# First double pair's q, k, v in a tile outside the pool that later holds odd batches' rows; SyncE's loads and stores also in the planned order

## The chip, the cores and the metric

One core of a Trainium2 chip. The time is device microseconds of one execution; the kernel before takes 632.27 us, median of 3 runs (630.27 to 633.63). TensorE multiplies matrices, ScalarE applies tanh and exp, VectorE adds, transposes in 32x32 blocks and normalises, GpSimd casts weights and gathers and scatters rows, SyncE issues the plain DMA transfers.

## The reference

```python
def _attn_ref(q, k, v, cap):                      # 8 batches, 12 heads, 448 rows, 64 wide
    scores = np.matmul(q, k.transpose(0, 1, 3, 2)) / np.sqrt(q.shape[-1])
    scores = cap * np.tanh(scores / cap)
    attn = np.exp(scores - np.max(scores, axis=-1, keepdims=True))
    attn = attn / (np.sum(attn, axis=-1, keepdims=True) + 1e-09)
    return np.matmul(attn, v)

def _moe_ref(x, w_gate, w1, w2, capacity):        # x: 8 x 448 x 768, w1 768 x 1024, w2 1024 x 768
    scores = np.einsum('bsd,d->bs', x, w_gate)
    out = x.copy()
    for b in range(B):
        top_idx = np.argpartition(-scores[b], capacity)[:capacity]      # 128 of 448 rows
        xe = x[b, top_idx]
        ye = np.maximum(xe @ w1, 0.0) @ w2
        g = 1.0 / (1.0 + np.exp(-scores[b, top_idx]))
        out[b, top_idx] = x[b, top_idx] + g[:, None] * ye
    return out
```

All arrays are float32. The attention output with its heads joined is x of the second part.

## The kernel before

The work on heads is cut into 24 "doubles" of two pairs of heads each, three doubles to a batch. A double has q and k tiles of 128 x 448 for each pair (lines 268 to 271), one v tile (273 to 275), and runs in 7 steps over 64 rows of k. A step is four scores products into a PSUM tile ps (L283), tanh on ScalarE into p (L321), exp in place (L324), four products of p with v into acc (L291), and an add of p into e on VectorE (L334). At a double's end TensorE sums e over partitions (sums, L368), VectorE transposes acc and the sums (L360, L376), takes reciprocals, normalises into xn, which holds a batch's rows (L406), and reduces the gate's scores (L428, L432). SyncE stores xn to the output in four transfers after a batch's second and again after its third double (L421). A float32 product shows as two matmul records in the trace, so a step of four scores products counts as x8.

When a batch's three doubles are done, VectorE and TensorE rank its 448 gate scores and pick 128 rows; GpSimd gathers them from the output (L550), the expert products run on TensorE in three parts each (L616, w1 then w2, split in high and low parts), and GpSimd scatters the result (L675). The weights come once, in 14 transfers into three staging tiles (L245), are cast by GpSimd (L248) and split by VectorE (L251).

A planner sets the order: each piece of work is a task with an engine, an assumed duration, a priority, and slots that it takes and gives (SIZES: 2 for "qk", 3 for "v", 2 for "S" in PSUM, 7 for "P", 2 for "xn"). `Plan.run` plays the tasks through and emits instructions in the order in which they would begin. Expert products are used as filling between attention steps; once no more than RESERVE = 42000 ns of them are left they are held until the attention products are done. On TensorE, ScalarE, VectorE and GpSimd the instructions stand in the order emitted (`manual_schedule`); SyncE's are not in that list before, and the tile framework's own scheduler orders them by priority and by when it expects the tiles to be free. On each engine instructions start in order, and SyncE's transfers wait in one line for the semaphores of the tiles that they overwrite.

The first double's loads are issued before the branch on the cap (`tc.If`), from the same pool and tags (`q0`, `k0`, ... with two buffers, `v` with three) as those of all later doubles.

Of the kernel before, what the change touches and what calls it, by code (L numbers as in the profile page):

```python
# [9 lines left out]
F32 = mybir.dt.float32  # L10
# [160 lines left out]
def load_flag(tc, K, cap):  # L171
    nc = tc.nc
    cp = K.const
    K.cap = cp.tile([P, 1], F32, name="capc")
    nc.sync.dma_start(K.cap, cap.to_broadcast([P, 1]))
    K.ident = cp.tile([P, P], F32, name="ident")
    make_identity(nc, K.ident)
    K.fast = cp.tile([1, 1], I32, name="fast")
    sq = cp.tile([1, 1], F32, name="sq")
    nc.vector.tensor_tensor(sq, K.cap[:1], K.cap[:1], op=ALU.mult)  # L180
    nc.vector.tensor_scalar(K.fast, sq, CAP_FAST * CAP_FAST, None, op0=ALU.is_le)
    K.sc = cp.tile([P, 1], F32, name="sc")
    nc.vector.reciprocal(K.sc, K.cap)
    nc.vector.tensor_scalar_mul(K.sc, K.sc, 1.0 / float(K.D) ** 0.5)
    nc.scalar.activation(sq, sq, AF.Tanh)
    K.wts = {}
    for nm, n, m in (("w1", K.ND, K.F), ("w2", K.NF, K.DM)):
        for part in "hl":
            K.wts[nm + part] = cp.tile([P, n, m], F32R, name=nm + part)
    K.wg = cp.tile([P, K.NG, 2, Q], F32, name="wg")  # L190
    K.iota = cp.tile([P, P], F32, name="iota")
    K.ids = cp.tile([P, K.NCH], F32, name="ids")
    K.vals = [cp.tile([P, 4, K.NCH], F32R, name=f"vals{i}") for i in range(2)]
    K.score = [cp.tile([P, K.NCH], F32, name=f"score{i}") for i in range(2)]
    K.rk = [cp.tile([P, K.NCH], F32, name=f"rk{i}") for i in range(2)]
    K.before = cp.tile([P, K.NCH * P], BF16, name="before")
    K.fold = cp.tile([P, 4, Q], F32, name="fold")
    K.ones = cp.tile([P, HD], F32, name="ones")
    K.hs = cp.tile([P, 1024], F32, name="hs")


def load_consts(tc, K):
# [57 lines left out]
class Double:  # L260
# [5 lines left out]

    def load_qk(self, tc, K, h, slot):
        for nm, src in (("q", K.q), ("k", K.k)):
            t = K.work.tile([P, K.S], F32, tag=f"{nm}{h}", name=nm, bufs=2)
            getattr(self, nm)[h] = t  # L270
            tc.nc.sync.dma_start(t, src[self.d, h])  # L271

    def load_v(self, tc, K, slot):
        self.v = K.work.tile([P, K.S // HD, 2, HD], F32, tag="v", name="v", bufs=3)
        tc.nc.sync.dma_start(self.v, K.v[self.d])


# [19 lines left out]
    D.acc = K.psV.tile([P, 2, 512], F32, tag="V", name="acc", bufs=1)  # L297


def attention_tasks(tc, K, D, loaded):  # L300
    nc = tc.nc
    add, S, NS = K.plan.add, K.S, K.NS
    g0 = D.d * NS
    lqk, lv = loaded
    if lqk is None:
        lqk = add("SP", 2400, lambda t: [D.load_qk(tc, K, h, t.got["qk"]) for h in range(2)],
                  prio=g0 - 12, take=("qk",), lat=3500)
        lv = add("SP", 700, lambda t: D.load_v(tc, K, t.got["v"]), prio=g0 - 11, take=("v",),
                 lat=4500)
    pv = prev = ex = None  # L310
    qks = []
    for s in range(NS):
        g = g0 + s
        box = {}

        def qk(t, s=s, box=box):
            box["ps"] = scores_mm(tc, K, D, s, t.got["S"])

        def tanh(t, s=s, box=box):
            D.P[s] = w_tile(K, [P, 2, S], F32, "P", t.got["P"], "p")  # L320
            nc.scalar.activation(D.P[s], box["ps"][:, :, :S], AF.Tanh, scale=K.sc)  # L321

        def exp(t, s=s):
            nc.scalar.activation(D.P[s], D.P[s], AF.Exp, scale=K.cap)  # L324

        def product(t, s=s):
            if s == 0:
                new_acc(K, D)
            attend(tc, K, D, s)

        def sum2(t, s=s):
            if s == 1:
                D.E = w_tile(K, [P, 2, S], F32, "E", t.got["E"], "e")
            nc.vector.tensor_tensor(D.E, D.P[0] if s == 1 else D.E, D.P[s], op=ALU.add)  # L334

        a = add("PE", 752, qk, [lqk], prio=g, take=("S",), mode="att",
                give=[("qk", lqk)] if s == NS - 1 else ())
        qks.append(a)
        blk = g // 2 * 4
        th = add("ACT", 1030, tanh, [a], prio=blk, take=("P",), give=[("S", a)])  # L340
        ex_ = add("ACT", 1075, exp, [th], prio=blk + 1)
        pv_ = add("PE", 752, product, [ex_, lv, pv], prio=g + 1.5, mode="att",
                  take=("V",) if s == 0 else (),
                  give=[("v", lv)] if s == NS - 1 else ())
        if s == 0:
            first_pv, first_th, first_ex = pv_, th, ex_
        else:
            sm_ = add("DVE", 1065, sum2, [ex_, prev if s > 1 else first_ex], prio=g + 2,
                      take=("E",) if s == 1 else ())
            done = add("NONE", 0, lambda t: None, [sm_, pv_], prio=-100, give=[("P", th)])  # L350
            if s == 1:
                first_sum = sm_
                add("NONE", 0, lambda t: None, [sm_, first_pv], prio=-100,
                    give=[("P", first_th)])
            prev = sm_
        pv = pv_
# [33 lines left out]
def output_tasks(tc, K, D, x, rc):  # L390
# [5 lines left out]
    def normalise(t):  # L396
        if grp == 0:
            K.xn_slot[b] = t
            K.xn[b] = w_tile(K, [P, NB, NG, 2, Q], F32, "xn", t.got["xn"], "xn")
            K.part[b] = w_tile(K, [P, NG, NB], F32, "part", t.got["xn"], "part")  # L400
        xn = K.xn[b][:, :, grp].rearrange("p b r d -> p r b d")
        xT = D.xT.rearrange("p r (b d) -> p r b d", d=Q)
# [340 lines left out]

def fast_path(tc, K, first, w1, w2):
    plan = K.plan
    weights(tc, K, w1, w2)
    for d in range(K.B * K.NG):
        D = first if d == 0 else Double(K, d)
        if d == 0:
            loaded = []  # L750
            for key in ("qk", "v"):
                loaded.append(plan.add("SP", 0, lambda t: None, prio=-1000, take=(key,),
                                       lat=1500))
        else:
            loaded = (None, None)
        x, rc = attention_tasks(tc, K, D, loaded)
        output_tasks(tc, K, D, x, rc)
        end_batch(tc, K, D)
    warm = K.bank(1)
    for _ in range(WARM):  # L760
        tc.nc.tensor.matmul(warm[:, :P], lhsT=K.ident, rhs=K.ident, start=True, stop=True)
    load_consts(tc, K)
    load_gate(tc, K)

    def after_attention():
        plan.free["bank"] += [2, 3, 4]

    plan.run(after_attention)
# [10 lines left out]
def main_kernel(ctx: ExitStack, tc: tile.TileContext, q, k, v, cap, w_gate, w1, w2, out, C, dims):  # L779
# [28 lines left out]
    K.bank = bank  # L808
    load_flag(tc, K, cap)
    first = Double(K, 0)  # L810
    first.load_qk(tc, K, 0, 0)
    first.load_qk(tc, K, 1, 0)
    first.load_v(tc, K, 0)
    fast = nc.values_load(K.fast[0:1, 0:1], min_val=0, max_val=1)
    with tc.If(fast > 0) as cmp:
        if C <= P:
            K.plan = Plan(SIZES)
            engines = {mybir.EngineType.PE, mybir.EngineType.Activation, mybir.EngineType.DVE,
                       mybir.EngineType.Pool}
            with tc.manual_schedule(engines=engines):  # L820
                fast_path(tc, K, first, w1, w2)
        else:
# [72 lines left out]
```

## Time and profile before

| what | value |
|---|---|
| runs of the kernel before | 630.27, 633.63, 632.27 us |
| profiled execution | 629.62 us |
| span of its instructions | 627.9 us |
| mean granted clock of TensorE | 0.906 of full speed |
| busy: TensorE, VectorE, ScalarE, GpSimd | 519.0, 399.6, 349.0, 41.2 us |
| moved by DMA | 57.41 MB |

The page gives busy shares per engine, the span in 40 slices, the chain of work that ended last and the costliest groups of instructions. In the views of the trace, a row of the timeline has the start in us from the span's start, the duration in us, engine, line, operation, output and inputs, the count of merged instructions, and in brackets the idle time before it with what ended it. SPq is SyncE's queue of transfers, PEld the weight loads of TensorE. Ends of matmuls are modelled and overlap the next start, so TensorE's pace is read from starts.

### The profile page before, as it was taken

The numbers are of one execution on the slowest core, as the hardware profiler recorded it, in microseconds if no ns is written. First come the engines' busy times: TensorE is split into PE (matmuls) and PEld (weight loads), VectorE is DVE, ScalarE is ACT, GpSimd is POOL, SyncE is SP. The second block draws the span as 40 slices with busy tenths as digits, with TensorE's granted clock in tenths as the row PEclk, the third lists the DMA queues.
The fourth block names the chain that finished last, engine by engine and source line by source line (L and its number), as shares of the span: only waits on it lengthen the run. The fifth ranks groups of instructions, "written<-read, shape, count | busy, mean of one in ns | idle before, by whom it ended". The sixth has DMA issues, their size and how long they took to land.

```text
span 627.9 us, 9365 instructions
## 1 busy us (share of the span) xinstructions
PE 519.0 (83%) x3750; PEld 262.4 (42%) x3750; DVE 399.6 (64%) x671; ACT 349.0 (56%) x394; POOL 41.2 (7%) x40
## 2 busy tenths in 40 slices
PE   6586975979779889799699789896799798795996
PEld 2131322524434435345254333353345344333896
DVE  2879465868576666696287574593748846868621
ACT  5766664638546563676466384663558556690110
POOL 1421001000010000200001000010000000010100
PEclk9888776979898898999799797897979989996999
DMA  7436333151331530342222432115313244103110
GB/s 241 171 110 182 83 105 111 54 143 36 112 99 40 148 89 31 109 130 76 60 88 82 117 77 72 58 58 167 88 33 89 71 128 116 62 25 80 42 45 29
DMA packets 50659, 57.41 MB, mean 91 GB/s; under 512 B 17968, under 2 KB 44720, under 8 KB 50608
## 3 DMA queue, kind: packets, MB, share of 16 engines
q1 hardware_dynamic: 49328, 50.44, 28.0%
q0 software_dynamic: 1280, 6.29, 3.0%
q8 instruction: 31, 0.51, 0.3%
q14 instruction: 20, 0.16, 0.1%
HBM read 42.57 MB, written 14.16 MB: 90 GB/s over the span
## 4 chain that ended last, share of the span: by engine, by line
PE 60%; DMA 16%; DVE 10%; issue 6%; SPq 4%; ACT 2%; POOLq 0%; DVEq 0%
PE ps L283 20%; PE pb L616 18%; PE acc L291 16%; DMA k<-in_k 15%; DVE e L334 5%; SPq L271 4%; PE sums L368 3%; PE pb L579 2%; DMA stage<-in_moe_w 1%; ACT p L321 1%; DVE xn L406 1%; DVE xT L360 1%; DVE sm L376 1%; PE pb L470 1%; ACT p L324 1%
## 5 line engine op out<-in xcount | busy, mean ns | idle before, releaser
L283 PE MATMUL ps<-q,k 64*64 64x448 f32 x1344 | 207.8, 600 | 80.8 <-DMA k<-in_k 79.0
L321 ACT ACTIVATE p<-ps,sc 128x896 f32<-128x896 f32 x168 | 165.9, 1005 | 185.8 <-PE ps L283 169.2
L291 PE MATMUL acc<-p,v 64*64 64x448 f32 x1344 | 180.9, 580 | 1.6 <-ACT p L324 0.6
L324 ACT ACTIVATE p<-p,capc 128x896 f32<-128x896 f32 x168 | 169.9, 1042 | 1.7
L334 DVE TENSOR_TENSOR e<-e,p 128x896 f32<-128x896 f32 x120 | 133.0, 1108 | 39.4 <-ACT p L324 34.1
L283 PEld LDWEIGHTS ps<-q,k 64*64 64x64 f32 x1344 | 62.8, 145 | 188.5 <-issue 103.1
L291 PEld LDWEIGHTS acc<-p,v 64*64 64x64 f32 x1344 | 54.7, 140 | 80.4 <-issue 56.3
L360 DVE STREAM_TRANSPOSE xT<-acc 128x896 f32<-128x896 f32 x24 | 26.7, 1112 | 56.8 <-PE acc L291 52.2
L368 PE MATMUL sums<-e,ones 64*64 64x448 f32 x192 | 27.5, 585 | 14.0 <-DVE e L334 14.0
L550 POOL DMA_INDIRECT xe<-out,idx x8 | 13.1, 1632 | 386.3 <-DVE gt L556 386.3
L376 DVE STREAM_TRANSPOSE sm<-sums 128x896 f32<-128x896 f32 x24 | 26.5, 1103 | 14.0 <-PE sums L368 14.0
L616 PE MATMUL pb<-w2h,hh 128*128 128x384 f32 x128 | 30.5, 356 | 1.1 <-DVE hl L586 1.1
L637 ACT ACTIVATE hs<-pb 128x512 f32<-128x512 f32 x16 | 9.4, 594 | 38.5 <-PE pb L616 38.4
L616 PE MATMUL pb<-w2h,hl 128*128 128x384 f32 x128 | 30.5, 357 | 0.0
L616 PE MATMUL pb<-w2l,hh 128*128 128x384 f32 x128 | 29.4, 346 | 0.0
L334 DVE TENSOR_TENSOR e<-p 128x896 f32<-128x896 f32 x24 | 26.0, 1083 | 5.1 <-ACT p L324 5.1
L616 PE MATMUL pb<-w1h,xl 128*128 128x512 f32 x96 | 27.5, 413 | 0.0
L666 DVE SCALAR_TENSOR_TENSOR xe<-pb,gt,xe 128x384 f32<-128x384 f32 x16 | 9.8, 615 | 27.3 <-PE pb L616 27.2
L616 PE MATMUL pb<-w1h,xh 128*128 128x512 f32 x96 | 27.0, 408 | 0.2 <-DVE xl L586 0.2
L616 PE MATMUL pb<-w1l,xh 128*128 128x512 f32 x96 | 27.1, 409 | 0.0
L406 DVE TENSOR_TENSOR xn<-xT,rec 128x896 f32<-128x896 f32 x24 | 26.5, 1106 | 0.6
L432 DVE TENSOR_REDUCE part<-jk 128x14 f32<-128x896 f32 x24 | 26.1, 1086 | 0.8
(76 smaller groups left out, 388.2 us busy)
## 6 DMA issues: line engine op xcount, KB each, us to landing
q<-in_q SPq DMA_DIRECT2D x48, 224.0 KB, 3.6
k<-in_k SPq DMA_DIRECT2D x48, 224.0 KB, 3.7
v<-in_v SPq DMA_DIRECT2D x24, 448.0 KB, 3.2
out<-xn SPq DMA_DIRECT2D x32, 224.0 KB, 3.6
out<-xn SPq DMA_DIRECT2D x32, 112.0 KB, 2.3
stage<-in_moe_w SPq DMA_DIRECT2D x6, 384.0 KB, 3.1
stage<-in_moe_w SPq DMA_DIRECT2D x4, 512.0 KB, 7.8
hs<-in_moe_w SPq DMA_DIRECT2D x2, 512.0 KB, 9.3
```

The source lines that it names most:

```text
L271: tc.nc.sync.dma_start(t, src[self.d, h])
L283: tc.nc.tensor.matmul(K.ps[HALF[r], j, :K.S], lhsT=D.k[r][HALF[j], ks], rhs=D.q[r][HALF[j], :], start=True, stop=True)
L291: tc.nc.tensor.matmul(D.acc[HALF[j], r, :K.S], lhsT=D.v[HALF[r], s, j, :], rhs=D.P[s][HALF[r], j, :], start=(s == 0), stop=(s == K.NS - 1))
L321: nc.scalar.activation(D.P[s], box["ps"][:, :, :S], AF.Tanh, scale=K.sc)
L324: nc.scalar.activation(D.P[s], D.P[s], AF.Exp, scale=K.cap)
L334: nc.vector.tensor_tensor(D.E, D.P[0] if s == 1 else D.E, D.P[s], op=ALU.add)
L360: nc.vector.transpose(D.xT, D.acc[:, :, :S])
L368: nc.tensor.matmul(D.sums[HALF[j], r, :S], lhsT=K.ones[HALF[r], :], rhs=D.E[HALF[r], j, :], start=True, stop=True)
L376: nc.vector.transpose(D.sm, D.sums[:, :, :S])
L406: nc.vector.tensor_tensor(xn, xT, D.rec.unsqueeze(3).to_broadcast([P, 2, NB, Q]), op=ALU.mult)
L432: nc.vector.tensor_reduce(K.part[b][:, grp, :], jk, axis=AX.X, op=ALU.add)
L616: nc.tensor.matmul(X["acc" + n_ops][:M, :ns[1]], lhsT=X[l][:, i, :M], rhs=K.wts[r][:, i, ns[2]], start=bool(start and n == 0), stop=(stop ...
```

## The change

The constants get one more tile, K.room, of 6 x 448 floats a partition. Double 0's two q, two k and its v are loaded into it (slot None). The later doubles' q, k and v are named by the planner's slot (`q00`, `q01`, ...), one buffer each, in place of a tag with two or three buffers. In the plan double 0 takes no slot of "qk" or "v". Of the two places for a batch's rows, the one for odd batches becomes K.room itself. The weights' tasks are added behind double 0's, not ahead, and SyncE joins the engines whose instructions stand in the planned order.

```diff
+    K.room = cp.tile([P, 6 * K.S], F32, name="room")
+    K.used = 0
+
+    def early(n):
+        K.used += n
+        return K.room[:, K.used - n:K.used]
...
     def load_qk(self, tc, K, h, slot):
         for nm, src in (("q", K.q), ("k", K.k)):
-            t = K.work.tile([P, K.S], F32, tag=f"{nm}{h}", name=nm, bufs=2)
+            if slot is None:
+                t = K.early(K.S)
+            else:
+                t = w_tile(K, [P, K.S], F32, f"{nm}{h}", slot, nm)
...
     def load_v(self, tc, K, slot):
-        self.v = K.work.tile([P, K.S // HD, 2, HD], F32, tag="v", name="v", bufs=3)
+        if slot is None:
+            self.v = K.early(K.S * 2).rearrange("p (s j d) -> p s j d", j=2, d=HD)
+        else:
+            self.v = w_tile(K, [P, K.S // HD, 2, HD], F32, "v", slot, "v")
...
-    lqk, lv = loaded
-    if lqk is None:
+    if D.d == 0:
+        lqk = add("NONE", 1500, lambda t: None)
+        lv = add("NONE", 0, lambda t: None)
+    else:
         lqk = add("SP", 2400, lambda t: [D.load_qk(tc, K, h, t.got["qk"]) for h in range(2)],
                   prio=g0 - 12, take=("qk",), lat=3500)
...
-                give=[("qk", lqk)] if s == NS - 1 else ())
+                give=[("qk", lqk)] if D.d and s == NS - 1 else ())
...
-            K.xn[b] = w_tile(K, [P, NB, NG, 2, Q], F32, "xn", t.got["xn"], "xn")
+            if t.got["xn"]:
+                K.xn[b] = K.room.rearrange("p (b g h d) -> p b g h d", g=NG, h=2, d=Q)
+            else:
+                K.xn[b] = w_tile(K, [P, NB, NG, 2, Q], F32, "xn", 0, "xn")
...
     plan = K.plan
-    weights(tc, K, w1, w2)
     for d in range(K.B * K.NG):
         D = first if d == 0 else Double(K, d)
+        x, rc = attention_tasks(tc, K, D)
+        output_tasks(tc, K, D, x, rc)
         if d == 0:
-            loaded = []
-            for key in ("qk", "v"):
-                loaded.append(plan.add("SP", 0, lambda t: None, prio=-1000, take=(key,),
-                                       lat=1500))
-        else:
-            loaded = (None, None)
-        x, rc = attention_tasks(tc, K, D, loaded)
-        output_tasks(tc, K, D, x, rc)
+            weights(tc, K, w1, w2)
         end_batch(tc, K, D)
...
-    first.load_qk(tc, K, 0, 0)
-    first.load_qk(tc, K, 1, 0)
-    first.load_v(tc, K, 0)
+    first.load_qk(tc, K, 0, None)
+    first.load_qk(tc, K, 1, None)
+    first.load_v(tc, K, None)
...
             engines = {mybir.EngineType.PE, mybir.EngineType.Activation, mybir.EngineType.DVE,
-                       mybir.EngineType.Pool}
+                       mybir.EngineType.Pool, mybir.EngineType.SP}
```

The first place is SyncE's queue after the branch. Before, with the buffers' numbers (wg is the gate's weight, stage and hs are staging tiles of w1):

```order
L774 DMA wg_89<-in_moe_w_gate 32x192 x4
L271 DMA q_154<-in_q 128x448
L271 DMA k_156<-in_k 128x448
L271 DMA q_158<-in_q 128x448
L271 DMA k_160<-in_k 128x448
L275 DMA v_172<-in_v 128x896
L275 DMA v_176<-in_v 128x896
L245 DMA stage_185<-in_moe_w1 128x1024
L245 DMA stage_187<-in_moe_w1 128x1024
L245 DMA hs_101<-in_moe_w1 128x1024
```

Double 1's q, k and v and double 2's v go out ahead of the weights. The same place in the change:

```order
L282 DMA q_150<-in_q 128x448
L282 DMA k_152<-in_k 128x448
L282 DMA q_154<-in_q 128x448
L282 DMA k_156<-in_k 128x448
L289 DMA v_168<-in_v 128x896
L282 DMA q_172<-in_q 128x448
L282 DMA k_174<-in_k 128x448
L282 DMA q_176<-in_q 128x448
L282 DMA k_178<-in_k 128x448
L289 DMA v_193<-in_v 128x896
L253 DMA stage_201<-in_moe_w1 128x1024
L253 DMA stage_211<-in_moe_w1 128x1024
```

Double 2's q and k moved ahead of the first weights; the weights keep their order behind.

The second place is SyncE's queue in the middle of the kernel. Before (out<-xn are stores, 32x14x128 after a batch's second double, 32x14x64 after its third):

```order
L421 DMA out<-xn 32x14x128 x3
L271 DMA q<-in_q 128x448
L271 DMA k<-in_k 128x448
L271 DMA q<-in_q 128x448
L271 DMA k<-in_k 128x448
L421 DMA out<-xn 32x14x128
L275 DMA v<-in_v 128x896
L421 DMA out<-xn 32x14x64 x4
```

Some of a double's four stores stand ahead of the next loads of q and k and some behind. In the change:

```order
L440 DMA out<-xn 32x14x128 x4
L282 DMA q<-in_q 128x448
L282 DMA k<-in_k 128x448
L282 DMA q<-in_q 128x448
L282 DMA k<-in_k 128x448
L289 DMA v<-in_v 128x896
L440 DMA out<-xn 32x14x64 x4
```

The four stores stand together ahead of the loads. Which double's tiles a load fills is not in these rows.

The third place is TensorE's queue at the end of the attention work. Before, from the last expert products (L616) ahead of the reserve to the first behind it:

```order
L616 MATMUL pb<-w1h,xl 128x512
L291 MATMUL acc<-p,v 64x448 x4
L283 MATMUL ps<-q,k 64x448 x4
L579 MATMUL pb<-ident,hs 128x128 x4
L470 MATMUL pb<-ident,score_94 128x128 x4
L283 MATMUL ps<-q,k 64x448 x4
L291 MATMUL acc<-p,v 64x448 x8
L283 MATMUL ps<-q,k 64x448 x8
L291 MATMUL acc<-p,v 64x448 x4
L283 MATMUL ps<-q,k 64x448 x4
L291 MATMUL acc<-p,v 64x448 x4
L283 MATMUL ps<-q,k 64x448 x4
```

One more run of two steps (x8, four products a step) follows before the expert products begin again: 8 scores steps in all. In the change, from the same kind of row:

```order
L635 MATMUL pb<-w1h,xl 128x512 x3
L305 MATMUL acc<-p,v 64x448 x4
L297 MATMUL ps<-q,k 64x448 x8
L305 MATMUL acc<-p,v 64x448 x4
L297 MATMUL ps<-q,k 64x448 x4
L598 MATMUL pb<-ident,hs 128x128 x4
L305 MATMUL acc<-p,v 64x448 x4
L297 MATMUL ps<-q,k 64x448 x8
L478 MATMUL pb<-score,fold 128x14
L305 MATMUL acc<-p,v 64x448 x8
L489 MATMUL pb<-ident,score_94 128x128 x4
L297 MATMUL ps<-q,k 64x448 x8
```

These hold 7 of 18 scores steps before the expert products (L635) return; the last expert product ahead of the reserve stands 10 steps earlier than before.

## Rows read from the trace of the kernel before

**Rows 1.** The page's first two parts: busy time of each engine with its share and count; granted clock of TensorE in tenths, and GB/s moved, in 40 equal slices.

```profile
PE 519.0 (83%) x3750; PEld 262.4 (42%) x3750; DVE 399.6 (64%) x671; ACT 349.0 (56%) x394; POOL 41.2 (7%) x40
PEclk9888776979898898999799797897979989996999
GB/s 241 171 110 182 83 105 111 54 143 36 112 99 40 148 89 31 109 130 76 60 88 82 117 77 72 58 58 167 88 33 89 71 128 116 62 25 80 42 45 29
```

**Rows 2.** The page's chain of work that ended last, shares of the span by line.

```profile
PE ps L283 20%; PE pb L616 18%; PE acc L291 16%; DMA k<-in_k 15%; DVE e L334 5%; SPq L271 4%; PE sums L368 3%; PE pb L579 2%; DMA stage<-in_moe_w 1%; ACT p L321 1%; DVE xn L406 1%; DVE xT L360 1%; DVE sm L376 1%; PE pb L470 1%; ACT p L324 1%
```

**Rows 3.** The view of waits over the whole span, TensorE's scores products: engine, line, what was waited for, us in total, times, longest.

```profile
PE ps L283 <- DMA k<-in_k: 79.0, 38, 7.0
```

**Rows 4.** The timeline of all engines at the boundary of two doubles.

```profile
300.15 0.93 PE L283 MATMUL ps<-q,k 64*64 64x448 f32 x8
...
301.13 0.36 SPq L271 DMA_DIRECT2D q<-in_q  x1
...
302.48 0.43 SPq L271 DMA_DIRECT2D k<-in_k  x1
...
304.39 0.98 PE L283 MATMUL ps<-q,k 64*64 64x448 f32 x4 [3.31 <-DMA k<-in_k]
...
306.81 1.01 PE L283 MATMUL ps<-q,k 64*64 64x448 f32 x2 [1.44 <-DMA k<-in_k]
```

**Rows 5.** Timelines of SyncE's queue and of TensorE in the first 43 us (the first 56 records of L283 are double 0's).

```profile
7.10 0.42 SPq L271 DMA_DIRECT2D q<-in_q  x1
...
39.03 0.33 SPq L271 DMA_DIRECT2D q<-in_q  x1
...
6.75 2.46 PE L283 MATMUL ps<-q,k 64*64 64x448 f32 x16
9.65 1.88 PE L283 MATMUL ps<-q,k 64*64 64x448 f32 x16 [0.44 <-ACT p L321]
...
13.30 1.88 PE L283 MATMUL ps<-q,k 64*64 64x448 f32 x16
...
16.95 1.98 PE L283 MATMUL ps<-q,k 64*64 64x448 f32 x16
...
37.31 1.69 PE L283 MATMUL ps<-q,k 64*64 64x448 f32 x16
```

**Rows 6.** The view of waits, SyncE's queue, columns as in rows 3.

```profile
SPq L421 <- DVE xn L406: 144.3, 16, 23.9
SPq L271 <- PE ps L283: 97.4, 16, 13.2
```

**Rows 7.** Busy time of each engine (and instructions) in three stretches: length, PE, PEld, DVE, ACT, POOL, granted clock, DMA share, GB/s.

```profile
6.75:118.70 111.95, 84.55 (x665) 29.59 (x665) 73.52 (x105) 72.03 (x79) 17.99 (x13) 0.83 0.43 133
118.70:560.25 441.55, 378.65 (x2778) 186.08 (x2781) 291.62 (x487) 264.36 (x296) 16.70 (x13) 0.92 0.30 85
560.25:627.90 67.65, 54.27 (x310) 45.41 (x302) 32.75 (x68) 11.09 (x18) 4.44 (x5) 0.91 0.18 51
```

**Rows 8.** Timelines of VectorE and GpSimd near the start.

```profile
12.38 1.09 DVE L334 TENSOR_TENSOR e<-p 128x896 f32<-128x896 f32 x1 [5.07 <-ACT p L324]
...
18.84 1.23 DVE L251 TENSOR_TENSOR w1l<-stage,w1h 128x1024 fp32r<-128x1024 f32 x1 [2.65 <-POOL w1h L248]
19.98 1.92 DVE L334 TENSOR_TENSOR e<-e,p 128x896 f32<-128x896 f32 x1
...
19.03 1.94 POOL L248 CAST w1h<-stage 128x1024 fp32r<-128x1024 f32 x1 [0.22 <-DMA stage<-in_moe_w]
```

**Rows 9.** The view of waits in the first two stretches of rows 7, first the first: TensorE's wait for k.

```profile
PE ps L283 <- DMA k<-in_k: 18.8, 7, 7.0
...
PE ps L283 <- DMA k<-in_k: 60.2, 31, 4.8
```

**Rows 10.** Two stretches of 16 us around rows 4, columns as in rows 7.

```profile
288.00:304.00 16.00, 13.08 (x104) 6.84 (x102) 10.37 (x14) 10.49 (x12) 0.00 (x0) 1.00 0.28 77
304.00:320.00 16.00, 14.17 (x94) 7.41 (x98) 5.68 (x10) 7.78 (x9) 0.00 (x0) 0.79 0.16 45
```

**Rows 11.** Timelines: TensorE where it alternates scores and values without a wait, and ScalarE where it goes from two steps' tanh to the next two's.

```profile
228.21 0.93 PE L283 MATMUL ps<-q,k 64*64 64x448 f32 x8
228.96 0.93 PE L291 MATMUL acc<-p,v 64*64 64x448 f32 x8
229.72 0.93 PE L283 MATMUL ps<-q,k 64*64 64x448 f32 x8
...
12.25 1.90 ACT L321 ACTIVATE p<-ps,sc 128x896 f32<-128x896 f32 x2
...
15.89 1.91 ACT L321 ACTIVATE p<-ps,sc 128x896 f32<-128x896 f32 x2
```

**Rows 12.** Timeline of SyncE's queue, two groups of stores.

```profile
422.75 0.86 SPq L421 DMA_DIRECT2D out<-xn  x2
...
444.88 1.92 SPq L421 DMA_DIRECT2D out<-xn  x4
```

**Rows 13.** Timeline of TensorE in the last stage.

```profile
559.10 1.69 PE L283 MATMUL ps<-q,k 64*64 64x448 f32 x16
...
573.67 1.77 PE L368 MATMUL sums<-e,ones 64*64 64x448 f32 x8 [6.77 <-DVE e L334]
...
621.51 0.86 PE L616 MATMUL pb<-w2h,hl 128*128 128x384 f32 x4
```

More of the change, by code (lines that the diff above doesn't have):

```diff
@@ L199, in load_flag @@
     K.hs = cp.tile([P, 1024], F32, name="hs")
+    K.room = cp.tile([P, 6 * K.S], F32, name="room")
[3 more added lines that the diff above has]
+        return K.room[:, K.used - n:K.used]
+    K.early = early
 def load_consts(tc, K):
@@ L297, in new_acc, with attention_tasks @@
     D.acc = K.psV.tile([P, 2, 512], F32, tag="V", name="acc", bufs=1)
-def attention_tasks(tc, K, D, loaded):
+def attention_tasks(tc, K, D):
     nc = tc.nc
@@ L309, in attention_tasks @@
                  lat=4500)
-    pv = prev = ex = None
+    pv = prev = None
     qks = []
@@ L343, in attention_tasks @@
                   take=("V",) if s == 0 else (),
-                  give=[("v", lv)] if s == NS - 1 else ())
+                  give=[("v", lv)] if D.d and s == NS - 1 else ())
         if s == 0:
```

## The prediction

> **What bounds the kernel now.** I read the page's first two parts, then the chain, then the waits, then the timeline at one place where a new double pair ("double", four heads of one batch) begins. TensorE is busy 83% of the span, VectorE 64%, ScalarE 56%, and TensorE's clock digit falls to 6 to 8 in many slices [rows 1]. So TensorE is nearest to being the bound, but a sixth of the span is idle and part of the rest runs at half clock. The chain says why: 15% of it is the landing of k, and 4% the issuing of these loads on SyncE [rows 2], together some 115 us in which the chain runs through no engine that computes. TensorE's largest wait by far is for k: 79.0 us in 38 waits [rows 3].
>
> The timeline of one boundary shows the mechanism [rows 4]. TensorE starts the last scores product of one double at 300.15; SyncE issues the next double's q and k at 301.13 to 302.48, straight after it; TensorE then idles 3.31 us, does half a step, and idles 1.44 more for the second k. The load was not late because of traffic: it was not issued until the double before had read its q and k. The start proves that [rows 5]. Double 1's q was issued at 7.10, and TensorE passed from double 0 to double 1 in the middle of the run that begins at 16.95 with no wait. Double 2's q went out only at 39.03, behind double 1's last scores run (37.31), though double 0's last step had passed in that same run at 16.95. Two buffers are declared, but the one that double 0 took before the branch never comes back; every later double shares one.
>
> SyncE's own waits say the same: 97.4 us of L271 for scores products, and 144.3 us of L421, the stores, for normalised rows [rows 6].
>
> **The change part by part.** (1) Double 0 goes to K.room, so doubles 1, 2, 3, ... alternate between two slots per tile that the planner hands out; double 3's load waits for double 1's last scores product, a whole double earlier than now. In the first place of the order both doubles 1 and 2 are loaded before any weight. (2) SyncE follows the planner: four stores stand together, where the scheduler put two or three ahead of the next loads and the rest behind. (3) The planner's input changes a little, so the other engines' orders change in detail. No computing instruction is added or removed. (4) Batch 1's first normalise writes where double 0's tiles were, so it waits for double 0's last products; three doubles lie between, which hide it, and without them it would cost VectorE at most one step.
>
> I sum over three stages, whose rows are one view [rows 7].
>
> Stage A, 6.75 to 118.70, before the first expert product: 111.95 us, TensorE busy 84.6, VectorE 73.5. There are no expert products to fill TensorE yet. If VectorE alone set the pace, from its first add at 12.38 [rows 8], the stage would end near 12.4 + 72.5 = 85 (about 1 us of the 73.5 lies before). If only TensorE's 18.8 us of waits for k in this stage [rows 9] went, it would end at 118.7 - 18.8 = 99.9. The new SyncE order puts four q and k tiles (224 KB each) and a v (448 KB) ahead of the first weights; at the 241 GB/s of the first slice [rows 1] that is 1344 KB or 5.7 us, and VectorE already waits 2.65 us for the first cast [rows 8]. So I stay near the upper end: 97. No change at all here would be 118.7.
>
> VectorE's add took 1.92 us at 19.98 beside a GpSimd cast of 1.94, against 1.09 for the add at 12.38 [rows 8]. [...]
>
> Stage B, 118.70 to 560.25, up to the last scores run: 441.55 us, of which TensorE is busy 378.65, so 62.9 idle; 60.2 of that is the wait for k [rows 7, 9]. The granted clock averages 0.92. [...] The half-clock time follows the stalls: 288 to 304 has 1.00, the next 16 us, which begin in the boundary shown above, 0.79 [rows 10].
>
> [...]
>
> So TensorE's own work in stage B is 441.55 - 62.9 - 35.3 = 343 us. VectorE's 291.6 and ScalarE's 264.4 in the same stage would then be 85% and 77% of it, so new waits appear that the stalls cover today. One is visible in the order: at the end the planner holds back some 42 us of expert work, and now the last 18 scores steps (8 before) have no expert products among them. Alone, TensorE needs 1.61 us a step (0.75 for scores, 0.75 for values by the starts, a seventh of 0.75 for sums), ScalarE 1.82 (3.64 for two steps) [rows 11]; 18 steps cost 0.2 x 18 = 4 us. For all new waits I take 15, between 0 and the 67 that would come if VectorE could only be kept busy at 0.71 of the stage. Stage B becomes 358.
>
> What hides the transfers then is a whole double of work: a load has some 15 us or more where it needs 4 (issue at 301.13, second half running by 306.81 [rows 4]). If that cover went, each double would pay its present wait again. In the new order SyncE's queue matters: q, k, v and stores wait in line. A store stands ahead of the loads of a later double, and waits for a normalise that comes within the next double; the loads behind it have a double in hand. I price that at 0, and at up to 1.9 us of issuing per group of four stores [rows 12] if the slack were gone.
>
> Stage C, 560.25 to the end: 67.65 us [rows 7]. TensorE's order there is the same: last sums at 573.67 after 6.77 us of wait for VectorE, then expert products without a gap to the last one at 621.5 [rows 13]. Nothing here loads q or k. I leave 67.65; the bounds are 6.8 less and, if VectorE is further behind, some 5 more.
>
> Sum: 97 + 358 + 67.7 = 523 us span. The profiled execution takes 629.62 with a span of 627.9, so 1.7 lie around it: 524.5. The median of before is 2.65 above that execution: **527 us**, 17% less.
>
> **The rivals.** *Other engines take the room.* The stalls are now VectorE's and ScalarE's time to catch up; when they go, TensorE waits for adds and activations instead. For it: VectorE at 85% of the new stage B, and 6.77 us of TensorE's waiting for adds where no load is due [rows 13]. Against: in stage B TensorE's idle time beside k is only 62.9 - 60.2 = 2.7 us. If VectorE manages 0.75 of stage B, that is 291.6 / 0.75 = 389, and with stage A at 105: 105 + 389 + 67.7 + 4.3 = 566 us.
>
> *Loads are held in SyncE's line.* If the loads that stand behind a store (two in three doubles) stay late, a third of the 105 us gain is left: 632 - 35 = 597. For it: the stores' 144.3 us of waits [rows 6]; against: these loads have a double in hand.
>
> *Slower.* The same line, decided at one point: a store's normalise ending later than the last scores product of the double before the one to be loaded. Then each such load is issued no earlier than now, and has four stores ahead of it (1.92 us) where it had two (0.86) [rows 12]: 16 x 1.06 = 17 us on top of today's 632, 649. It would need VectorE more than a double behind, always; today the longest single wait of a store is 23.9 us [rows 6], about what a double takes in stage B (441.55 us for some 18 doubles).
>
> *It doesn't do what it says*: if the slots of q and k still came back one double late, the waits would stay as they are: 632.
>
> **How the numbers follow.** The forecast has 0.74, with its own range 500 to 550 (stage A between 85 and 105, new waits between 0 and 30). Other engines 0.17 (566), held in line 0.05 (597), no change 0.02, slower 0.02. The range 503 to 572 leaves out held in line, no change and slower, and a tail of the forecast. A measurement of this kernel can tell about 0.5% from no change. Faster by more 0.96, within 0.5% 0.02, slower by more 0.02.
>
> **What would show it.** Right: TensorE's wait for k under 10 us and gone from the chain; q's issues about one double ahead of their use; a clock of 0.95 or more in stage B; a first expert product between 90 and 105; VectorE's and ScalarE's shares up to some 75% and 65% with the same busy times. Wrong: a wait for k of tens of us (the line), a new wait of TensorE for p or e of tens of us (other engines), or a clock that stays near 0.92 with the stalls gone.

## The result, and the profile after

The changed kernel takes 497.53 us (median of 4 runs, 497.22 to 498.8) where the kernel before takes 632.95 in the same series (4 runs, 630.27 to 636.8): a ratio of 0.786, 95% interval 0.782 to 0.791. It is 21% faster. The forecast was 527 us with a range of 503 to 572, so the time lies 29.5 us below the forecast and 5.5 below the range's low end: the direction and the mechanism came out as written, the size did not. One execution is left out of all numbers below: the kernel with one tile of q and k (further down) once took 2247 us, with 2337 ns in the mean for a record of its scores products where the execution shown further down has 595, against 619.74 to 626.65 us in ten others, and why is open.

The profiled execution takes 497.39 us with a span of 495.7. First the page of the changed kernel, the lines that answer to [rows 1, 2]: busy times, granted clock, GB/s, and the chain by line.

```profile
PE 463.2 (93%) x3750; PEld 243.3 (49%) x3750; DVE 399.9 (81%) x671; ACT 346.8 (70%) x394; POOL 43.0 (9%) x40
PEclk9988999999999999999999999999999999989998
GB/s 212 337 85 177 204 191 132 113 141 173 56 153 47 180 96 39 176 128 96 112 103 105 158 75 74 176 95 130 112 70 119 176 112 34 0 75 70 33 32 38
PE pb L635 25%; PE acc L305 18%; PE ps L297 16%; DVE e L350 7%; PE sums L384 4%; ACT p L337 2%; PE pb L598 1%; DVE jk L447 1%; DMA xe<-out,idx 1%; DMA stage<-in_moe_w 1%; DVE part L451 1%; DVE sm L392 1%; ACT p L340 1%; DVE jk L502 1%; DMA q<-in_q 1%
```

VectorE and ScalarE have the busy time they had, to 2.2 us. TensorE has 56 us less of it for the same 3750 records, and its idle time went from 109 us (627.9 - 519.0) to 32.5. The landing of k, 15% of the chain before, is no longer among its lines; VectorE's adds, e, rose from 5% to 7%.

The three stages are cut at the same events as in [rows 7]: up to the first expert product, up to the last scores run, and the rest. Columns: length, then busy time of PE, PEld, DVE, ACT and POOL, granted clock, DMA share, GB/s.

```profile
6.60:93.01 86.41, 74.62 (x657) 24.29 (x657) 73.23 (x104) 70.39 (x77) 18.41 (x13) 0.96 0.62 189
93.01:432.23 339.22, 335.71 (x2807) 173.85 (x2811) 296.43 (x494) 266.27 (x301) 18.55 (x13) 1.00 0.39 108
432.23:495.70 63.47, 51.36 (x288) 43.85 (x280) 28.50 (x62) 8.68 (x14) 3.94 (x4) 0.95 0.17 49
```

The middle stage is 102 us shorter, the first 25.5, the last 4.2. In the middle TensorE now idles 3.5 us in all, at full clock throughout; VectorE is busy 87% of it.

Next the boundary of two doubles in the changed kernel, in the timelines of SyncE's queue and TensorE (start, duration, engine, line, what), to be read against [rows 4].

```profile
235.87 0.36 SPq L282 DMA_DIRECT2D q<-in_q  x1
...
255.40 0.93 PE L297 MATMUL ps<-q,k 64*64 64x448 f32 x8
256.15 0.93 PE L305 MATMUL acc<-p,v 64*64 64x448 f32 x8
256.91 1.68 PE L297 MATMUL ps<-q,k 64*64 64x448 f32 x16
...
256.36 0.33 SPq L282 DMA_DIRECT2D q<-in_q  x1
```

The step at 255.40 is the last of one double, the run of two steps at 256.91 the first of the next, with one values' step between and no wait. Its q had been issued at 235.87, behind the last scores run of the double before that; the issue at 256.36 is for the double after. A load is thus issued one whole double, 21 us here, ahead of its use.

The view of waits, SyncE's queue, for [rows 6]; TensorE's list there has no wait for k any more.

```profile
SPq L282 <- PE ps L297: 111.0, 16, 14.0
SPq L440 <- DVE room L425: 71.9, 8, 29.2
SPq L440 <- DVE xn L425: 47.0, 8, 12.3
```

SyncE still waits 111 us for scores products and 118.9 (71.9 + 47.0) for rows. Before, its wait for scores products stood in the path, now it does not. The same row of a queue can be the fault or be nothing; what decides is whether TensorE waits for what comes out of it.

### The profile page after: what moved, and what is told of

It is laid out like the page before. It is cut to its first block, busy times and chain, and to the rows that moved or that the text cites. A ratio compares the mean times of both kernels' runs of the same rounds, so it can differ in the third digit from the quotient of the medians.

```text
span 495.7 us, 9354 instructions
## 1 busy us (share of the span) xinstructions
PE 463.2 (93%) x3750; PEld 243.3 (49%) x3750; DVE 399.9 (81%) x671; ACT 346.8 (70%) x394; POOL 43.0 (9%) x40
## 4 chain that ended last, share of the span: by engine, by line
PE 65%; DVE 19%; issue 5%; DMA 4%; ACT 4%; POOLq 0%; POOL 0%; DVEq 0%
PE pb L635 25%; PE acc L305 18%; PE ps L297 16%; DVE e L350 7%; PE sums L384 4%; ACT p L337 2%; PE pb L598 1%; DVE jk L447 1%; DMA xe<-out,idx 1%; DMA stage<-in_moe_w 1%; DVE part L451 1%; DVE sm L392 1%; ACT p L340 1%; DVE jk L502 1%; DMA q<-in_q 1%
## 5 line engine op out<-in xcount | busy, mean ns | idle before, releaser
L305 PE MATMUL acc<-p,v 64*64 64x448 f32 x1288 | 147.5, 552 | 2.0 <-ACT p L340 1.6
L297 PE MATMUL ps<-q,k 64*64 64x448 f32 x1288 | 145.4, 542 | 3.1 <-ACT p L337 1.8
L297 PEld LDWEIGHTS ps<-q,k 64*64 64x64 f32 x1288 | 47.3, 133 | 80.5 <-issue 34.6
L305 PEld LDWEIGHTS acc<-p,v 64*64 64x64 f32 x1288 | 44.6, 134 | 71.8 <-issue 46.6
L384 PE MATMUL sums<-e,ones 64*64 64x448 f32 x192 | 24.3, 577 | 12.1 <-DVE e L350 11.9
L656 ACT ACTIVATE hs<-pb 128x512 f32<-128x512 f32 x16 | 9.5, 598 | 35.3 <-PE pb L635 34.6
L635 PE MATMUL pb<-w2l,hh 128*128 128x384 f32 x128 | 30.6, 349 | 0.0
L635 PE MATMUL pb<-w2h,hl 128*128 128x384 f32 x128 | 29.8, 346 | 0.0
L635 PE MATMUL pb<-w2h,hh 128*128 128x384 f32 x128 | 29.1, 350 | 0.5 <-DVE hl L605 0.5
L635 PE MATMUL pb<-w1h,xh 128*128 128x512 f32 x96 | 27.6, 409 | 0.0
L635 PE MATMUL pb<-w1h,xl 128*128 128x512 f32 x96 | 27.2, 405 | 0.0
L635 PE MATMUL pb<-w1l,xh 128*128 128x512 f32 x96 | 26.1, 400 | 0.0
L635 PEld LDWEIGHTS pb<-w2h,hh 128*128 128x128 f32 x128 | 22.9, 192 | 5.1 <-issue 2.4
L635 PEld LDWEIGHTS pb<-w2h,hl 128*128 128x128 f32 x128 | 22.4, 189 | 2.8 <-issue 2.8
```

The source lines that it names most:

```text
L297: tc.nc.tensor.matmul(K.ps[HALF[r], j, :K.S], lhsT=D.k[r][HALF[j], ks], rhs=D.q[r][HALF[j], :], start=True, stop=True)
L305: tc.nc.tensor.matmul(D.acc[HALF[j], r, :K.S], lhsT=D.v[HALF[r], s, j, :], rhs=D.P[s][HALF[r], j, :], start=(s == 0), stop=(s == K.NS - 1))
L384: nc.tensor.matmul(D.sums[HALF[j], r, :S], lhsT=K.ones[HALF[r], :], rhs=D.E[HALF[r], j, :], start=True, stop=True)
L635: nc.tensor.matmul(X["acc" + n_ops][:M, :ns[1]], lhsT=X[l][:, i, :M], rhs=K.wts[r][:, i, ns[2]], start=bool(start and n == 0), stop=(stop ...
L656: nc.scalar.activation(K.hs[:M, fs], X["acc" + nm][:M], AF.Relu)
```

## The experiments

**Only the tiles, SyncE's order left to the scheduler.**

```diff
-                       mybir.EngineType.Pool, mybir.EngineType.SP}
+                       mybir.EngineType.Pool}
```

> The changed kernel with SyncE left to the tile framework's own scheduler again; room and slots by number stay. Theory (the loads are released a whole double earlier because two slots really alternate): 495 to 505 us, TensorE's wait for k under 5 us. Rival (it is the planned order of SyncE's queue that brings the loads early): 540 to 632 us with tens of us of waits for k.

Measured: 498.88 us (498.42 to 501.29), ratio to the kernel before 0.795 [0.788, 0.802]. TensorE has no wait for k in its profile. The gain is there without SyncE's planned order, which brings nothing that can be told from noise: the times differ by 1.35 us, and the intervals of the two ratios overlap. What is left is the room, the changed plan and the second tile; the next run takes the tile away.

**The same with one tile for each q and k of the later doubles, the planner not told.**

```diff
-                t = w_tile(K, [P, K.S], F32, f"{nm}{h}", slot, nm)
+                t = w_tile(K, [P, K.S], F32, f"{nm}{h}", 0, nm)
```

> As e1, but q and k of all doubles after the first have one tile each, which the planner does not know of; everything else of the change stays (room for odd batches, weights' tasks behind double 0's). Theory: back to 620 to 640 us, with 70 to 85 us of TensorE waiting for k and a mean granted clock near 0.91. Rival (the plan's other changes give a part of the gain): under 610 us.

Measured: 622.3 us (median of ten runs, 619.74 to 626.65), ratio 0.992 [0.988, 0.996]. So this kernel, which has K.room and the changed plan but a single tile, is within 1% of the kernel before: the room and the plan bring some 0.8% (0.4 to 1.2), the second tile the rest of the 21%. It fits the reading of [rows 5], that two buffers were declared and one worked.

The places of the tiles in the built programs say the same outright. In the kernel before, double 0's first q lies at byte 110624 of each partition, and the first q of all 23 later doubles at byte 112416. In the changed kernel the later doubles alternate between 121376 and 135712, and in this one all of them lie at 121376. That the branch is the reason no run here shows; in a build of the kernel before with double 0's loads moved inside the branch, which was not timed, q alternates between 110624 and 112416, so that smaller change is an untried rival to this one.

The profile of this kernel comes from one more execution:

> The kernel of the run with one tile for q and k of the later doubles, looked at once more for its profile. If the gain of the change lies in the second tile alone, this profile has the mechanism of before in it: TensorE waits for k some 70 to 85 us in 36 to 40 waits, SyncE's loads of q and k wait for TensorE's last scores product of the double before, granted clock 0.90 to 0.92, time 618 to 628 us. Rival (the room and the plan's new input do something of their own): a wait for k under 50 us at the same time, with another wait in its place.

Measured: 618.88 us, clock 0.915. Its waits and one of its boundaries:

```profile
PE ps L297 <- DMA k<-in_k: 76.5, 25, 7.9
...
299.00 0.97 PE L297 MATMUL ps<-q,k 64*64 64x448 f32 x4 [2.54 <-DMA k<-in_k]
301.16 1.75 PE L297 MATMUL ps<-q,k 64*64 64x448 f32 x4 [1.19 <-DMA k<-in_k]
```

The wait, the half step and the second wait of [rows 3, 4] are back, though the 76.5 us come in 25 waits where 36 to 40 were named. The rival, that the room or the plan's new input does much of its own, falls, but for the 0.8% above.

**One slot, and the planner told of it.** In the changed kernel:

```diff
-SIZES = {"qk": 2, "v": 3, "S": 2, "V": 1, "P": 7, "E": 2, "xT": 2, "sm": 1, "rec": 2, "xn": 2,
+SIZES = {"qk": 1, "v": 3, "S": 2, "V": 1, "P": 7, "E": 2, "xT": 2, "sm": 1, "rec": 2, "xn": 2,
```

> The changed kernel with one planner slot for q and k instead of two: the planner knows of the late release and can put expert products into the gaps. Theory (the stall is a hole in TensorE's order that other work could fill): 530 to 590 us, TensorE's wait for k well under 79 us. If the hole can't be filled, because the planner's lead time for a load is shorter than the load or no expert products are ready: 600 to 640 us.

Measured: 538.34 us (535.66 to 539.6), ratio 0.857 [0.850, 0.864], clock 0.989. From the page, the waits and one boundary of this kernel:

```profile
PE 483.2 (91%) x3750; PEld 238.4 (45%) x3750; DVE 401.1 (75%) x671; ACT 346.2 (65%) x394; POOL 43.6 (8%) x40
...
PE ps L297 <- DMA k<-in_k: 2.4, 3, 0.9
PE acc L305 <- ACT p L340: 16.5, 19, 1.7
...
241.43 0.93 PE L297 MATMUL ps<-q,k 64*64 64x448 f32 x8
242.29 0.97 PE L635 MATMUL pb<-w2h,hh 128*128 128x384 f32 x4
242.38 0.36 SPq L282 DMA_DIRECT2D q<-in_q  x1
...
248.97 0.93 PE L297 MATMUL ps<-q,k 64*64 64x448 f32 x8
```

This kernel has the same single tile of q and k as the run before it, and 84 us less time. The load is as late as ever, issued at 242.38 behind the last scores step of the double before (241.43), but the planner knows it, and puts expert products into the gap: the next double's first step comes at 248.97 without a wait, and the wait for k is 2.4 us in all. Before, the planner counted on two slots that the pool did not give; it placed the first scores step of a double straight behind the last one [rows 4], and nothing of TensorE's started until k had come. Two things differ from the one-tile run, the planner's slots and SyncE's planned order; with two tiles that order was worth nothing measurable, with one tile it was not tried alone. By the ratios, some 14 of the 21% saved are thus the end of a wrong assumption, and some 7 are the second tile itself.

**The clock held up.** The kernel before, with 14 products of the identity in the gap ahead of the first scores step of doubles 2 and later, written to the PSUM tile that the step overwrites:

```diff
+    if s == 0 and D.d > 1:
+        for _ in range(14):
+            tc.nc.tensor.matmul(K.ps[:, 0, :P], lhsT=K.ident, rhs=K.ident, start=True, stop=True)
```

> The kernel before with 14 products of the identity ahead of the first scores product of each double from 2 on, written to the scores tile that is overwritten after: they fill the wait for k and keep TensorE active. If the half clock after the stalls costs what the prediction took (35 us in stage B and some 5 more): 590 to 600 us with a mean clock over 0.97. If the busy time at half clock was partly the first half step that only waits for the second k: about 605 to 615. If half clock costs nothing because other engines set the pace then: 630 to 640, by the products' own time.

Measured: 612.85 us (607.31 to 618.9), ratio 0.975 [0.967, 0.983], 15.5 us less, clock 0.97 in place of 0.91; the second of the three expectations. With 14 products more at each of these boundaries the kernel is faster, at the higher mean clock. The gain is under the 35 us that the prediction took for the middle stage alone. But at 0.97 the clock is still short of 1.00, and the 14 products take time of their own (3.39 us at a boundary of the profiled execution, from 291.99), so for what the clock costs I take 15.5 as a lower bound, an estimate.

**Waiting for both halves at once.** The kernel before, with the second pair's products first in the first step of doubles 2 and later:

```diff
-    for r in range(2):
+    for r in ((1, 0) if s == 0 and D.d > 1 else (0, 1)):
```

> Kernel before, with the second pair's two products ahead of the first pair's in the first scores step of doubles 2 and later, so TensorE waits for the last k at once. Theory (in the kernel before, the half step that TensorE does between the two waits at a boundary only passes time that it would wait anyway, since the second half of the step ends as late either way plus half a step at most): time within 1% of before, 627 to 640 us; the wait for k becomes one per boundary, about 22 of them, and longer in all by 15 to 25 us, with TensorE's busy time smaller by as much. Rival (the first half step is work of its own that the second wait doesn't hide): 15 to 20 us slower, 648 to 652 us.

Measured: 637.99 us (635.5 to 639.93), ratio 1.0135 [1.008, 1.019]; inside the theory's 627 to 640 us, but not within 1% of before. From its page, its waits and a boundary, which is that of [rows 4]:

```profile
PE 504.0 (79%) x3750; PEld 275.2 (43%) x3750; DVE 399.5 (63%) x671; ACT 349.0 (55%) x394; POOL 40.8 (6%) x40
...
PE ps L283 <- DMA k<-in_k: 105.4, 22, 8.3
...
303.06 0.93 PE L283 MATMUL ps<-q,k 64*64 64x448 f32 x8
309.51 1.88 PE L283 MATMUL ps<-q,k 64*64 64x448 f32 x8 [5.51 <-DMA k<-in_k]
311.32 1.11 PE L579 MATMUL pb<-ident,hs 128*128 128x128 f32 x4
```

and the kernel before, behind the second wait of [rows 4]:

```profile
308.50 0.90 PE L579 MATMUL pb<-ident,hs 128*128 128x128 f32 x3
```

From the last step of a double to the first work behind the new double's first step it is 308.50 - 300.15 = 8.35 us before and 311.32 - 303.06 = 8.26 here: at this boundary the half step done early brought nothing. Over the kernel the wait for k is 105.4 us in place of 79.0, 26.4 more, in an execution whose span is 10.3 longer (638.2 against 627.9), and TensorE is busy 504.0 us in place of 519.0 for the same 3750 records. So some 15 us that the page of before lists as busy were wait, as the theory said. The 10.3 are not divided; part of them may be the clock, 0.892 here and 0.906 before.

**VectorE made slower.** In the changed kernel, the reduction of the gate's scores done twice:

```diff
         nc.vector.tensor_reduce(K.part[b][:, grp, :], jk, axis=AX.X, op=ALU.add)
+        nc.vector.tensor_reduce(K.part[b][:, grp, :], jk, axis=AX.X, op=ALU.add)
```

> Changed kernel, with the reduction of the gate's scores done twice in each double: 24 x 1.09 = 26 us more of VectorE, planner unaware. Theory (TensorE sets the pace of the changed kernel's middle stage, and VectorE only that of its first, where it is busy 85%, and of its tail): 5 to 8 of the reductions show, 503 to 507 us. Rival (VectorE is the bound beside TensorE now that the stalls are gone): 20 us or more, 518 to 524 us. A time between says what share of VectorE's work lies on the path.

Measured: 511.7 us (510.55 to 512.43), 14.2 above the changed kernel, for some 24 us of added work (VectorE busy 423.8 in place of 399.9); neither expectation. The middle stage, columns as above:

```profile
97.67:444.50 346.83, 338.45 (x2812) 175.10 (x2816) 315.78 (x513) 266.69 (x301) 18.28 (x13) 1.00 0.38 106
```

The first stage ends 4.7 us later, the middle one takes 7.6 more for some 19 us of added work, with TensorE's idle time in it up from 3.5 to 8.4. TensorE still bounds the middle stage, but VectorE is close behind: two fifths of the work added there show, and more than half over the kernel. The "other engines" rival was wrong for this change, and is next in line.

**The weights first.** In the changed kernel, double 2's load of q and k put behind the first weight's:

```diff
-                  prio=g0 - 12, take=("qk",), lat=3500)
+                  prio=8.5 if D.d == 2 else g0 - 12, take=("qk",), lat=3500)
```

> Changed kernel, but double 2's load of q and k has a priority behind the first weight's load, so the first weights go out ahead of it as before. It prices what the prediction allowed for the weights' delay (stage A to end at 97 where 93 to 94 follows without the delay). Theory (the first cast comes only 1.07 us later in the changed kernel than before, and VectorE has other work meanwhile): within 0.3% of the changed kernel, 496 to 499 us. Rival (the delay of the weights costs several us): 492 to 494 us.

Measured: 497.45 us (496.42 to 497.94), the changed kernel's time. The first cast comes at 17.29 here, where the changed kernel has it at 18.84, and nothing follows from it: the first expert product starts at 93.82, against 93.01. The delay of the weights costs nothing that shows, as the theory said.

**The tail.** In the changed kernel TensorE waits for VectorE at the end of the attention work, while 42 us of expert products are held back:

```profile
434.82 1.92 PE L305 MATMUL acc<-p,v 64*64 64x448 f32 x16 [1.30 <-ACT p L340]
441.23 1.43 PE L384 MATMUL sums<-e,ones 64*64 64x448 f32 x8 [4.49 <-DVE e L350]
```

Three kernels tried that place. One lets the held products go when only the last sums are left:

```diff
-        if self.att_left and self.heavy_left <= RESERVE:
+        if self.att_left > 1 and self.heavy_left <= RESERVE:
             heavy = []
+        if self.att_left == 1 and att:
+            return first(att)
```

> Changed kernel, with the held expert products let go once only the last sums are left of the attention products, so that some 3.5 us of them fill TensorE's wait for VectorE's last add (4.5 us in the changed kernel's profile). Theory (TensorE's own work is what is left, so idle time filled is time gained, if the held work still covers the last batch's selection): the last sums start after no wait, 492 to 495 us. Rival (the last batch's chain on VectorE and GpSimd ends as late as before, and TensorE only idles later, in front of the last batch's transposes): 497 to 498 us, with a new idle time of 3 to 5 us near 465.

The second has RESERVE = 48000 as well:

> The same with 48 us of expert products held in place of 42, so that the last selection stays covered though some go ahead of the last sums. Theory: 490 to 493 us, TensorE without idle time between the last values' product and the last expert product. Rival (steps without expert products among them cost more than the planner's filling brings): 497 us or more, with waits of TensorE for p in the steps before the end.

The third has RESERVE = 36000 and no other edit:

> Changed kernel with 36 us of expert products held in place of 42. The middle stage has them as filling, so its last steps are nearer to TensorE's pace: with 0.2 us a step lost in steps without filling (what the prediction took), about 4 steps fewer give back 0.8 us; against it the last batch's selection is covered for 6 us less. Theory (TensorE has 23 us of held products ahead of the last batch's transposes, all needed): 3 to 6 us slower, 500 to 504 us, idle in front of those transposes. Rival (the selection had slack): 496 to 498 us.

Measured: 493.07 us (490.77 to 494.58) for the first, 494.58 (493.76 to 496.95) for the second, 497.37 (494.91 to 498.7) for the third; ratios to the kernel before 0.784, 0.787 and 0.790, each within 0.004 to either side. The first in the timeline of TensorE:

```profile
434.51 1.92 PE L307 MATMUL acc<-p,v 64*64 64x448 f32 x16 [1.31 <-ACT p L342]
436.36 0.96 PE L637 MATMUL pb<-w2h,hh 128*128 128x384 f32 x4
...
440.91 0.98 PE L386 MATMUL sums<-e,ones 64*64 64x448 f32 x8 [0.81 <-DVE e L352]
```

Five groups of expert products stand in the gap, the wait is 0.81 us instead of 4.49, and the sums take 0.98 instead of 1.43: the granted clock from 436 to 445 is 1.00, against 0.81 in the changed kernel's 436.4 to 445.4. Behind the sums' start its span has 49.2 us (490.1 - 440.91) where the changed kernel has 54.5; the five groups, some 3.5 us, are what moved ahead of it. Its median is 4.3 us below the third kernel's on the same chip, and the fastest measured here; the intervals of the ratios overlap, so "about 1% faster than the change" is what can be said. The first theory's 492 to 495 us came out, the second's 490 to 493 did not: with 48 us held the sums start at 437.73, but nothing more is won. In the third, TensorE comes to the last batch's transposes (at 472.43) without idle time, so the reserve had slack, and the rival was right there.

## Why the prediction was wrong by 29 us

**What held.** The buffer that double 0 took before the branch was not used again; giving double 0 its own tile, and the later doubles tiles by slot, made the two slots real; TensorE's wait for k went from 79.0 us to none; the loads go out a double ahead; the middle stage's clock rose from 0.92 to 1.00; the first expert product came at 93.0 (90 to 105 were named); the transfers found their cover, and SyncE's line took none of it back. VectorE's and ScalarE's shares of the span rose past the 75% and 65% named, to 81% and 70%, since the span came out shorter.

**What failed** was the size, term by term; the sum of 527 lies 29.5 us above 497.5.

1. *New waits in the middle stage*, taken as 15, measured as 339.22 - 335.71 = 3.5: 11.5 us. The term stood between 0 and 67, and 15 was chosen because VectorE would be at 85% of the stage. VectorE is now at 87% of it and TensorE hardly waits for it: p has 7 slots and expert products lie between the steps, which I take for the reason (argued, not tried). The rival *other engines take the room* fell for the same reason; the run with more VectorE work shows that it had only a little room left.

2. *TensorE's own work in the middle stage*, worked out as 343, measured as 335.7: 7.3 us. For the same records the miss is some 10, because this stage now holds 29 records more (2807 against 2778), about 2.7 us if each takes 0.094 [rows 11, eight records in 0.75 us], an estimate: 333. The step that failed is "441.55 us, of which TensorE is busy 378.65, so 62.9 idle". Listed busy time, less a share for the clock, was taken as work. Between its two waits at a boundary TensorE did half a step that needs 0.38 us at full clock (half of 0.75), and that was listed with 0.98 [rows 4], before it waited again. In the middle stage the listed busy time holds 378.65 - 333 = 45.7 us that is no work, and the prediction allowed 35.3 for it, all of it clock. No run shows that 35.3.

What a granted clock of 0.50 costs shows in the trace of before from 25.34 to 35.57, where the clock is 0.50 throughout:

```profile
31.56 1.75 PE L291 MATMUL acc<-p,v 64*64 64x448 f32 x8
33.06 1.75 PE L283 MATMUL ps<-q,k 64*64 64x448 f32 x8
34.55 1.45 PE L291 MATMUL acc<-p,v 64*64 64x448 f32 x8
```

The starts are 1.50 and 1.49 us apart, twice the 0.75 of [rows 11]. The trace of before divides the 45.7, too. In the middle stage its granted clock is 0.50 in 13 stretches; here is their sum in the view of stretches, the length and then busy time by engine:

```profile
sum 68.26, PE 59.41 PEld 23.07 DVE 8.92 ACT 19.64 POOL 0.00; mean PE 4.57 PEld 1.77 DVE 0.69 ACT 1.51 POOL 0.00
```

TensorE is listed busy in 59.4 of these 68.3 us. By the starts above, half of that, 29.7, is the most that the clock can have cost, an estimate; the prediction's 35.3 charged it for idle time too. So some 16 at least are not clock. The run that waits for both halves at once agrees, with 15 us of listed busy time that turn out to be wait over the whole kernel. The run that holds the clock up gives back 15.5 over the whole kernel; as a lower bound it fits, and decides nothing here.

The granted clock of the middle stage was 0.92 before, with 60.2 us of waits for k [rows 7, 9], and is 1.00 in the changed kernel, without them; that was worth at most the 29.7 us.

3. *Stage A*, taken to end at 97, ended at 93.0: 4 us. "I stay near the upper end" rested on the weights' delay behind four q and k tiles. These rows of the changed kernel, GpSimd's first cast and VectorE's work around it, answer to [rows 8]:

```profile
18.84 1.04 POOL L256 CAST w1h<-stage 128x1024 fp32r<-128x1024 f32 x1 [12.38 <-DMA stage<-in_moe_w]
...
19.92 1.23 DVE L259 TENSOR_TENSOR w1l<-stage,w1h 128x1024 fp32r<-128x1024 f32 x1 [2.29 <-POOL w1h L256]
21.06 3.77 DVE L350 TENSOR_TENSOR e<-e,p 128x896 f32<-128x896 f32 x2
```

VectorE waits 2.29 us for the first cast, where it waited 2.65 before. The run with the weights first shows no such cost. What ends the stage is another thing, which neither bound of the prediction held: the chain of work that ends last goes through VectorE more than through any other engine up to 84.25, near the 85 worked out for VectorE alone; there GpSimd starts the gather of the first expert rows, and its landing (6.92 us), six transposes and a values step stand before the first expert product at 93.01. The two adds at 21.06 take 1.89 us each in the mean, beside casts of 1.92 (at 20.13) and 1.35 (at 22.53), as the add at 19.98 in [rows 8] took 1.92 beside its cast; an add of the same form at 81.94, with GpSimd idle, takes 1.08.

4. *Stage C*, left at 67.65, took 63.5: 4.2 us. The wait for the last add is 4.49 instead of 6.77, which is 2.3. Most of the rest is work that changed sides: 22 records, some 2.1 us at 0.094 each, now stand ahead of the cut (288 against 310: one double's sums, one step's values and six transposes) and are among the 29 more of the middle stage. "TensorE's order there is the same" was not so. The bound of 6.8 less had been named and not used.

5. *The step from the profiled execution to the median*, 2.65 us: the execution shown lies 0.14 below the median here, so 2.5 us more.

All five lie on one side, which the range had no room for: its low end moved two of them alone (stage A between 85 and 105, waits from 0), while the own work and the tail stood fixed. With the waits at 0 and stage A at its end of 85 the sum would have been 500, and with the tail's bound 493; the range began at 503.

The *slower* rival (loads behind late stores) and *held in line* fell together: SyncE waits 118.9 us in front of its stores, 25 less than before, and no load that TensorE needs comes late for it. *It doesn't do what it says* fell by the issue at 235.87.

## What to carry to other kernels

Where a plan counts on buffers, prove from the trace that they come back: a load that is issued only behind the last reader of the double just before it, whatever the declaration says, either has one buffer or is held in its queue, and the tiles' addresses in the built program tell the two apart. A planner that knows of one buffer (538 us) is worth more than a kernel with a plan for two that has one (622 us), so check the plan's assumptions before more memory is spent. When a stall is priced, look for wait in the busy time on both sides of it, a half step between two waits above all, and add the clock; then let the range take all fixed terms to their bounds together, since they can err to one side together, as here.

## What was not expected of the hardware

Adding 14 products without use at each of 22 boundaries shortens the kernel by 2.5%, with a mean granted clock of TensorE of 0.97 of full speed in place of 0.91. And TensorE at 99% of a stage of 339 us leaves VectorE 87% and ScalarE 78% busy beside it with 3.5 us of waits in all, which the prediction had thought too dense to go without 15.
